# Threshold attention and a mixture of attention experts on one core: the same instructions from a new order table

## The chip, the core and the metric

The kernel runs on one core of a Trainium2 chip. The core has TensorE (PE in the profile; PEld is its weight load), VectorE (DVE), ScalarE (ACT), GpSimd (POOL) and SyncE (SP), which here only issues DMAs. ACT issues a few DMAs too. The engines run side by side, each works through its own list in order, and they wait for one another by semaphores. The metric is the device time of one execution in microseconds (us). Kernels are compared by the medians of their runs.

## The reference, cut to what matters

```python
# batch 8, heads 8, sequence S = 576, head_dim 64
scores = scale * q @ k.T                             # per batch and head
thresh = max(scores, -1) - tau                       # tau = 0.02
scores = where(scores >= thresh, scores, -1e9)
attn   = exp(scores - max); attn /= sum + 1e-9
x      = (attn @ v), heads side by side              # 8 x 576 x 512
logits = x @ w_gate                                  # 4 experts, the best 2 are used
for e in range(4):
    q, k, v = x @ wq[e], x @ wk[e], x @ wv[e]        # 512 -> 64
    a  = causal softmax(scale * q @ k.T)
    ye = a @ v @ wo[e]                               # 64 -> 512
    out += (weight of expert e in this row) * ye
```

All inputs and outputs are float32. The weights wq and wk are large (64 times the usual), so the products that lead to scores are computed in split precision.

## The kernel before, in words

The 64 heads are worked through as 32 pairs of two heads (n = 0 to 31). After every fourth pair one batch is complete, and its second half (projections, gate, expert attention, output) is put between the pairs that follow.

**One pair.** q and k are loaded (`ldq`, `ldk`: eleven DMAs a pair into one `qi` and one `ki` buffer, so the loads of pair n+1 wait until the transposes of pair n have read them), transposed on PE into PSUM (`tq`, `tk`, lines 1240 and 1103), and copied out as a high part rounded for the PE's fp32r mode and a low part (`kh`, `kl`, `qh`, `ql`; lines 1142, 1079 to 1087, 1155). For pairs 1 to 5 this takes three steps: a raw copy, a cast (line 1079, 1081 or 1083) and two halves of a subtraction (line 1087), which may run on POOL. The rows are then cut into five query tiles. A tile has a score matmul (`s`, names kk and qq, line 1103), and per head: the row minimum with a copy out of PSUM (`min`, DVE, line 1203), the exponential (`exp`, ACT, line 1216), the threshold with multiply and row sum (`stt`, DVE, line 1220), the reciprocal (DVE, line 1231), the scaling of the 576 columns (`pn`, line 1498 on POOL or DVE, 1496 on ACT), the transposition on PE (`tm`, line 1240), its copy out of PSUM (`pt`, line 1079 ACT or 1081 DVE), and the product with v (`av`). A small add (`thr`, `eps1`) stands ahead of stt and of the reciprocal (line 1074 DVE, 1211 ACT, 1213 POOL).

**One batch's second half.** x is split into high and low parts (`xh`, `xl`, `xd`), projected to q2 and k2 (`pj`) and to values and gate logits (`v`), the gate is computed in small steps, then causal scores (`s2`, `s2t`), row minimum (line 1470), exponential (1475, 1490), scaling (`p2s`), transposition (`t2`, line 1093), product with the values (`bv`), and the output projection with its store (`o`, `ob`, `st`).

**The weights** (`w`, `wh`, `wl`: load, cast to the high part, subtraction for the low part) are prepared beside the first four pairs; wo is woh and wol in the profile.

**What sets the order.** Nothing is ordered by loops. `work()` makes about 5,300 tasks, each with a name. `ORDER` gives each task its place, a number in one list over all engines, and `BY` gives the engine, as a digit, to each task that may run on several:

```python
by = int(BY[family][i]) if len(t) > 1 else 0
x = Task({...}, fn, deps, takes, uses, cols, ld, name, ORDER[family][i], by)
for t in sorted(tasks, key=lambda t: t.place):       # in plan()
```

`plan()` goes through the tasks by place, gives each its buffer, and emits them in that order; so the place decides where a task stands in the list of its engine. While the PE is still cold it also puts small matmuls on a constant (`tri`) between tasks, to keep it busy. The digits: for copies out of PSUM (`pt`, `kh`, `xr`) 0 is ACT and 1 is DVE; for casts (`xh`, `wh`, `qd`) 0 is POOL, 1 ACT, 2 DVE; for scalings (`pn`, `p2s`) 0 is POOL, 1 DVE, 2 ACT; for small adds and fences 0 is DVE, 1 ACT, 2 POOL; for subtractions (`xl`, `wl`, `kl`, `ql`) 0 is POOL and 1 is DVE.

Of the kernel before, what the change touches and what calls it, by code (L numbers as in the profile page):

```python
# [248 lines left out]
def work(K):  # L249
# [320 lines left out]
    for n in range(NPR):  # L570
# [18 lines left out]
        12,  # L589
    ],  # L590
    "tau": [
        11, 18, 20,
    ],
    "w": [
        397, 498, 508, 259, 198, 278, 281, 25, 21, 29, 227, 142, 271, 354, 555, 22, 460, 495, 79, 233, 357, 406, 568, 358, 384, 362, 471, 302, 335, 484,
    ],
    "wh": [
        552, 547, 299, 30, 61, 280, 180, 35, 502, 133, 319, 410, 447, 500,
    ],
    "wl": [  # L600
        574, 565, 331, 41, 109, 355, 246, 37, 505, 226, 336, 430, 462, 532,
    ],
    "ldk": [
# [7 lines left out]
    ],  # L611
    "ldq": [
# [6 lines left out]
    ],  # L619
    "ldv": [  # L620
# [20 lines left out]
    "qh": [
        15, 19, 62, 152, 300, 677, 618, 709, 776, 387, 531, 612, 835, 1321, 1329, 1389, 1466, 930, 1239, 1370, 1524, 1936, 1966, 2094, 2038, 1665, 1815, 2006, 2168, 2590, 2640,
        2744, 2795, 2307, 2502, 2574, 2864, 3311, 3294, 3367, 3395, 3037, 3192, 3334, 3399, 3951, 4019, 4048, 4085, 3746, 3800, 3979, 4101, 4587, 4569, 4670, 4694, 4258, 4503,
        4593, 4740, 5106, 5117, 5178, 5172,
    ],
# [8 lines left out]
    ],  # L654
    "fs": [
        33, 122, 240, 367, 516, 637, 806, 986, 1142, 1258, 1471, 1710, 1736, 1890, 2111, 2356, 2374, 2626, 2732, 2999, 3071, 3259, 3431, 3682, 3798, 3837, 4078, 4248, 4421, 4548,
        4697, 4885,
    ],
    "min": [
# [300 lines left out]
    "fs2t": "2202220211021222",  # L960
    "zh": "000100000000010000010010100000110000000101000010",
    "fo": "112010000110111122222002101101200100",
    "ob": "000001000000000100100000010000110000",
}


# [623 lines left out]
```

## Time and profile before

| | us |
|---|---|
| median of 3 runs | 817.98 (817.97 to 818.85) |
| the profiled execution | 816.84 |
| its span, first to last instruction | 815.1 (1.7 lie around it) |
| busy in the span: PE / PEld | 791.2 / 731.0 |
| DVE / ACT / POOL | 730.3 / 697.7 / 423.3 |
| TensorE's mean granted clock | 0.998 |

Busy time is the time in which an engine had at least one instruction in work. Matmuls are pipelined and their ends are modelled, so PE's busy time holds short waits; PEld shows them better. The chain of waits follows the work that ended last back to the start. Idle time of an engine that is not on it costs nothing.

### The profile page before, as it was taken

The numbers are of one execution on the slowest core, as the hardware profiler recorded it, in microseconds if no ns is written. First come the engines' busy times: TensorE is split into PE (matmuls) and PEld (weight loads), VectorE is DVE, ScalarE is ACT, GpSimd is POOL, SyncE is SP. The second block draws the span as 40 slices with busy tenths as digits, with TensorE's granted clock in tenths as the row PEclk, the third lists the DMA queues.
The fourth block names the chain that finished last, engine by engine and source line by source line (L and its number), as shares of the span: only waits on it lengthen the run. The fifth ranks groups of instructions, "written<-read, shape, count | busy, mean of one in ns | idle before, by whom it ended". The sixth has DMA issues, their size and how long they took to land.

```text
span 815.1 us, 34755 instructions
## 1 busy us (share of the span) xinstructions
PE 791.2 (97%) x14117; PEld 731.0 (90%) x14117; DVE 730.3 (90%) x2331; ACT 697.7 (86%) x1449; POOL 423.3 (52%) x811
## 2 busy tenths in 40 slices
PE   9888999999999999999999999999999999999998
PEld 7777898899988999888998999889998899988997
DVE  6999989998989989898989988998999988999584
ACT  5989888997899868998899988999999987999475
POOL 5998625753445345544365435455345563468232
PEclk9999999999999999999999999999999999999999
DMA  4433212112132112222222122202311212220002
GB/s 115 89 80 72 66 38 45 42 45 52 39 83 55 37 47 50 55 64 52 46 54 64 43 73 55 61 14 69 80 42 38 67 45 50 59 55 3 15 27 80
DMA packets 140240, 44.21 MB, mean 54 GB/s; under 512 B 135216, under 2 KB 135216, under 8 KB 140080
## 3 DMA queue, kind: packets, MB, share of 16 engines
q1 hardware_dynamic: 138512, 41.65, 20.9%
q8 instruction: 111, 1.82, 1.0%
q10 hardware_dynamic: 1568, 0.34, 0.2%
q14 instruction: 49, 0.40, 0.2%
HBM read 32.51 MB, written 9.44 MB: 51 GB/s over the span
## 4 chain that ended last, share of the span: by engine, by line
PE 76%; DVE 9%; ACT 6%; POOL 5%; issue 3%; DMA 1%; SPq 0%; DVEq 0%; ACTq 0%; POOLq 0%
PE ps L1103 64%; PE ps L1240 10%; DVE e L1203 3%; PE ps L1093 3%; POOL e L1498 2%; DVE e L1220 2%; ACT pt L1079 1%; ACT e L1216 1%; DMA ki<-in_k_dram 1%; ACT e L1475 1%; DVE e L1470 1%; POOL sm L1213 1%; ACT pa L1079 0%; DVE pt L1081 0%; ACT e L1490 0%
## 5 line engine op out<-in xcount | busy, mean ns | idle before, releaser
L1498 POOL TENSOR_SCALAR e<-e,sm 128x576 f32<-128x576 f32 (+4 forms) x277 | 193.5, 708 | 82.0 <-DVE sm L1231 55.3
L1203 DVE TENSOR_SCALAR_CACHE_REDUCE e<-ps 128x576 f32<-128x576 f32 x288 | 209.5, 752 | 21.2 <-PE ps L1103 15.5
L1216 ACT ACTIVATE e<-e,sm 128x576 f32<-128x576 f32 x288 | 215.3, 771 | 10.9 <-DVE e L1203 8.8
L1220 DVE SCALAR_TENSOR_TENSOR e<-e,sm,e 128x576 f32<-128x576 f32 x256 | 209.4, 841 | 2.4 <-ACT e L1216 0.7
L1103 PE MATMUL ps<-kk,qq 64*128 64x288 f32 x1900 | 176.1, 309 | 5.7 <-POOL kk L1087 1.3
L1103 PEld LDWEIGHTS ps<-kk,qq 64*128 64x128 f32 x1900 | 139.9, 186 | 16.1 <-DVE e L1203 3.4
L1079 ACT ACTIVATE pt<-ps 128x640 f32<-128x640 f32 (+3 forms) x228 | 142.5, 639 | 13.1 <-PE ps L1093 5.4
L1103 PE MATMUL ps<-pt,vm 128*64 128x128 f32 (+1 forms) x1536 | 143.9, 259 | 0.0
L1240 PE MATMUL ps<-ident,e 64*128 64x64 f32 x2624 | 123.8, 226 | 7.1 <-DVE e L1203 2.7
L1103 PEld LDWEIGHTS ps<-pt,vm 128*64 128x64 f32 x1536 | 127.3, 137 | 2.7 <-issue 0.7
L1240 PEld LDWEIGHTS ps<-ident,e 64*128 64x128 f32 x2624 | 108.8, 139 | 19.1 <-issue 5.1
L1103 PE MATMUL ps<-pa,vm 128*64 128x128 f32 x1024 | 124.4, 274 | 0.0
L1103 PEld LDWEIGHTS ps<-pa,vm 128*64 128x64 f32 x1024 | 110.7, 137 | 3.3 <-issue 1.2
L1103 PE MATMUL ps<-x,wh 64*128 64x288 f32 x1024 | 106.0, 296 | 0.0
L1213 POOL TENSOR_TENSOR sm<-sm 128x2 f32<-128x2 f32 (+1 forms) x127 | 41.9, 333 | 121.7 <-DVE e L1220 82.5
L1496 ACT ACTIVATE e<-e,sm 128x576 f32<-128x576 f32 (+4 forms) x116 | 83.2, 730 | 5.9 <-DVE sm L1231 4.8
L1103 PEld LDWEIGHTS ps<-x,wh 64*128 64x128 f32 x1024 | 84.2, 185 | 0.6 <-ACT kk L1142 0.2
L1103 PE MATMUL ps<-x,wl 64*128 64x288 f32 x512 | 78.5, 292 | 0.0
L1475 ACT ACTIVATE e<-e,sm 128x384 f32<-128x384 f32 (+3 forms) x128 | 70.9, 557 | 1.6 <-DVE sm L1470 1.0
L1079 ACT ACTIVATE pa<-ps 128x512 f32<-128x512 f32 x105 | 62.2, 595 | 7.0 <-PE ps L1240 6.8
L1470 DVE CUSTOM_DVE_ANT_0 e<-ps,tri 128x384 f32<-128x384 f32 (+3 forms) x128 | 58.4, 484 | 3.7 <-PE ps L1103 2.9
L1359 POOL TENSOR_SCALAR fencePOOL<-eps 128x2 f32<-128x2 f32 x56 | 16.7, 298 | 83.5 <-PE ps L1103 80.1
(153 smaller groups left out, 1656.5 us busy)
## 6 DMA issues: line engine op xcount, KB each, us to landing
vm<-in_v_dram SPq DMA_DIRECT2D x64, 128.0 KB, 2.6
out_dram<-ob SPq DMA_DIRECT2D x32, 256.0 KB, 2.4
ki<-in_k_dram SPq DMA_DIRECT2D x63, 80.0 KB, 2.5
qi<-in_q_dram SPq DMA_DIRECT2D x63, 80.0 KB, 2.5
ki<-in_k_dram SPq DMA_DIRECT2D x63, 64.0 KB, 2.4
vt<-in_v_dram SPq DMA_DIRECT2D x128, 16.0 KB, 2.2
qi<-in_q_dram SPq DMA_DIRECT2D x31, 64.0 KB, 2.4
qi<-in_q_dram SPq DMA_DIRECT2D x31, 48.0 KB, 2.4
```

Source lines behind the costliest of these rows:

```text
L1079: self.nc.scalar.activation(dst, src, AF.Copy)
L1093: self.nc.tensor.transpose(self.ps[:, bank, c * n:(c + 1) * n], x[sl], self.ident[sl, sl])
L1103: return self.nc.tensor.matmul(out, x, y, start=first, stop=last)
L1203: self.nc.vector.tensor_scalar(self.sides(sc), self.dbank(s)[:, :, :HS], 0.0, None, op0=ALU.add, op1=ALU.min, accum_out=self.small(sm)[:, ...
L1213: self.nc.gpsimd.tensor_tensor(m[:, to:to + n], m[:, of:of + 2 * n:2], m[:, of + 1:of + 2 * n:2], op=ALU.add)
L1216: self.nc.scalar.activation(self.row(e), self.row(sc), AF.Exp, bias=self.small(sm)[:, 2 * j:2 * j + 1], scale=-1.0)
L1220: self.nc.vector.scalar_tensor_tensor(self.row(e), self.row(sc), m[:, 8 + j:9 + j], self.row(e), op0=ALU.is_le, op1=ALU.mult, accum_out=m[ ...
L1240: self.nc.tensor.transpose(self.ps[:, g.slot + h, c * D:(c + 1) * D], x, self.ident[sl, sl])
L1470: self.nc.vector.tensor_tensor_reduce(self.row(p2)[:, :w], self.dbank(g)[:, j, :w], self.tri[:, SM - w:], 1.0, FAR, op0=ALU.add, op1=ALU.m ...
L1475: self.nc.scalar.activation(p, p, AF.Exp, bias=m[:, 2 * j:2 * j + 1], scale=-1.0, accum_out=m[:, 4 + 2 * j:5 + 2 * j])
L1496: self.nc.scalar.activation(p, p, AF.Copy, scale=x)
L1498: (self.nc.vector if e == "DVE" else self.nc.gpsimd).tensor_scalar(p, p, x, 0.0, op0=ALU.mult, op1=ALU.add)
```

## The change

The tables `ORDER` and `BY` have new numbers; every other line is the same. Of `ORDER` nearly every row differs, by a few places for most tasks (6 on average for a score matmul, 14 for a scaling) and by more for loads and stores. Of `BY` some 640 digits differ. The start of the diff, and its short rows:

```diff
     "warm": [
-        12,
+        16,
     ],
     "tau": [
-        11, 18, 20,
+        10, 19, 28,
     ],
...
 BY = {
-    "tau": "100",
-    "wh": "11011002211000",
-    "wl": "00000011000000",
+    "tau": "000",
+    "wh": "10111110101000",
+    "wl": "10000000000010",
...
-    "kh": "011002100001000100000100000000001",
+    "kh": "001100100000000100000110000010010",
...
-    "kl": "000000010000000000000000000000000000",
+    "kl": "000001000100000000000000000000000000",
```

By instructions, before and now: DVE 1,757 and 1,735; ACT 1,313 and 1,328; POOL 816 and 823; SP 599 and 599; PE the same 11,928 matmuls, and 89 and 93 small ones on `tri`. The 576-column scalings are 25 and 9 on DVE, 187 and 200 on POOL, 92 and 95 on ACT. The 512-column copies `pa` are 23 and 32 on DVE, 105 and 96 on ACT.

Three places are shown as they stand in the engine's list. The first is the start of DVE's list, from the copies of the first pair's q (qq) to the first row minima (L1203). Before:

```order
L1081 COPY qq_1_180<-ps 128x320
L1042 TENSOR_SCALAR sm<-tau_t 128x8x2
L1144 TENSOR_SCALAR kk_4_195<-ps,qsc 128x320
L1081 CAST woh<-ob_3_193 128x512
L1087 TENSOR_TENSOR wol<-ob_3_193,woh 128x512
L1203 TENSOR_SCALAR e_6_231,sm<-ps 128x576 x2
L1074 TENSOR_REDUCE sm<-sm 128x2
```

Now:

```order
L1081 COPY qq_2_190<-ps 128x320
L1042 TENSOR_SCALAR sm<-tau_t 128x8x2
L1203 TENSOR_SCALAR e_6_217,sm<-ps 128x576 x2
L1074 TENSOR_REDUCE sm<-sm 128x2
L1220 SCALAR_TENSOR_TENSOR e_7_236,sm<-e_6_217,sm,e_7_236 128x576
```

The scaled copy of kk went to ACT, which now does both halves in a row, and the cast and the subtraction of one half of wo (woh, wol) went to POOL.

The second is DVE's list at the end of the fourth pair, ahead of the 36th and last stt (L1220) of the first batch. x is that batch's split x, iv the copy that it is made from, wh the high part of a weight. Before:

```order
L1498 TENSOR_SCALAR e_99_1421<-e_99_1421,sm 128x576
L1203 TENSOR_SCALAR e_104_1468,sm<-ps 128x576 x2
L1081 CAST x_109_1510<-iv_95_1367 128x320
L1081 CAST wh_120<-ob_98_1408 128x256
L1220 SCALAR_TENSOR_TENSOR e_106_1500,sm<-e_96_1371,sm,e_106_1500 128x576
L1081 CAST x_109_1510<-iv_102_1449 128x256
L1220 SCALAR_TENSOR_TENSOR e_106_1500,sm<-e_96_1371,sm,e_106_1500 128x576
```

Now:

```order
L1081 COPY pa_102_1443<-ps 128x512
L1231 RECIPROCAL sm<-sm 128x2
L1203 TENSOR_SCALAR e_105_1490,sm<-ps 128x576
L1074 TENSOR_REDUCE sm<-sm 128x2
L1203 TENSOR_SCALAR e_105_1490,sm<-ps 128x576
L1220 SCALAR_TENSOR_TENSOR e_101_1427,sm<-e_97_1400,sm,e_101_1427 128x576 x2
```

The scaling, the three casts and other pieces left DVE here; a copy of pa came.

The third is POOL's list at the subtractions for the fourth pair's kk (kk_61, the low part of k). wh and wl are weights. Before:

```order
L1087 TENSOR_TENSOR kk_61_918<-pt_53_821,kk_61_918 128x320
L1213 TENSOR_TENSOR sm<-sm 128x2
L1087 TENSOR_TENSOR qq_63_936<-pt_50_787,qq_63_936 128x320
L1498 TENSOR_SCALAR e_58_870<-e_58_870,sm 128x576
L1087 TENSOR_TENSOR wl_125<-ob_54_823,wh_122 128x256
L1083 TENSOR_SCALAR wh_122<-sm 128x4
L1087 TENSOR_TENSOR wl_125<-ob_47_760,wh_122 128x256
L1083 TENSOR_SCALAR x_72_1030<-iv_71_1026 128x256
L1087 TENSOR_TENSOR kk_61_918<-pt_53_821,kk_61_918 128x320
```

Now:

```order
L1083 TENSOR_SCALAR kk_61_914<-pt_55_873 128x640
L1213 TENSOR_TENSOR sm<-sm 128x1
L1083 TENSOR_SCALAR wh_122<-sm 128x4
L1083 TENSOR_SCALAR qq_66_973<-pt_47_778 128x640
L1087 TENSOR_TENSOR qq_66_973<-pt_47_778,qq_66_973 128x320
L1087 TENSOR_TENSOR kk_61_914<-pt_55_873,kk_61_914 128x320
L1087 TENSOR_TENSOR qq_66_973<-pt_47_778,qq_66_973 128x320
```

Before, seven other pieces stood between the two halves of kk; now POOL does one half, close behind the cast, and the other half is on DVE.

In SP's list the six loads of the fifth pair's k end at place 72 before and at place 68 now; before, the last three stood right behind three loads of the same pair's q.

## Rows read from the trace of the kernel before

**Rows 1.** The page: span; busy us of each engine (share of the span), instructions.

```profile
span 815.1 us, 34755 instructions
...
PE 791.2 (97%) x14117; PEld 731.0 (90%) x14117; DVE 730.3 (90%) x2331; ACT 697.7 (86%) x1449; POOL 423.3 (52%) x811
```

**Rows 2.** Busy us of each engine by stretch, TensorE's granted clock, DMA share, GB/s.

```profile
core 0: us, PE busy (x) PEld busy (x) DVE busy (x) ACT busy (x) POOL busy (x), PEclk, DMA share, GB/s
...
40.00:62.00 22.00, 18.55 (x309) 16.18 (x306) 20.19 (x59) 18.29 (x33) 21.82 (x33) 0.92 0.39 86
100.00:760.00 660.00, 651.53 (x11888) 605.14 (x11887) 610.08 (x1969) 586.30 (x1227) 329.99 (x641) 1.00 0.21 50
```

**Rows 3.** The chain that ended last: shares of the span by engine.

```profile
PE 76%; DVE 9%; ACT 6%; POOL 5%; issue 3%; DMA 1%; SPq 0%; DVEq 0%; ACTq 0%; POOLq 0%
```

**Rows 4.** Columns as in rows 2: the first batch after its start.

```profile
24.00:61.00 37.00, 31.52 (x545) 27.55 (x543) 34.39 (x96) 33.00 (x61) 36.54 (x50) 0.96 0.38 84
61.00:90.00 29.00, 24.95 (x458) 21.71 (x454) 28.54 (x77) 24.83 (x45) 24.82 (x36) 0.99 0.31 69
```

**Rows 5.** The chain in order of time (start, us, what), 78 to 81 us.

```profile
77.79 0.62 DVE x L1081
78.41 0.41 DVE wh L1081
78.82 0.73 DVE e L1220 x2
79.56 0.74 DVE x L1081
80.30 0.74 DVE e L1220 x2
```

**Rows 6.** DVE's timeline: start us, us, line, operation, tiles [idle before <-releaser].

```profile
8.02 0.55 DVE L1144 TENSOR_SCALAR kk<-ps,qsc 128x320 f32<-128x320 f32 x1
8.81 0.43 DVE L1081 CAST woh<-ob 128x512 fp32r<-128x512 f32 x1 [0.26 <-DMA ob<-in_moe_wo_dram]
9.28 0.69 DVE L1087 TENSOR_TENSOR wol<-ob,woh 128x512 fp32r<-128x512 f32 x1
9.88 0.75 DVE L1203 TENSOR_SCALAR_CACHE_REDUCE e<-ps 128x576 f32<-128x576 f32 x1
```

**Rows 7.** Groups by line and form: busy us, mean ns of one | idle before <-releasers.

```profile
L1220 DVE SCALAR_TENSOR_TENSOR e<-e,sm,e 128x576 f32<-128x576 f32 x256 | 209.4, 841 | 2.4 <-ACT e L1216 0.7
...
L1498 POOL TENSOR_SCALAR e<-e,sm 128x576 f32<-128x576 f32 x187 | 144.4, 780 | 68.2 <-DVE sm L1231 55.3 <-DVE sm L1074 5.2 <-PE ps L1103 3.4
...
L1079 ACT ACTIVATE pa<-ps 128x512 f32<-128x512 f32 x105 | 62.2, 595 | 7.0 <-PE ps L1240 6.8
...
L1081 DVE COPY pa<-ps 128x512 f32<-128x512 f32 x23 | 15.6, 684 | 2.5 <-PE ps L1240 2.5
...
L1498 DVE TENSOR_SCALAR e<-e,sm 128x576 f32<-128x576 f32 x25 | 13.3, 535 | 0.3
...
L1081 DVE CAST kk<-pt 128x640 fp32r<-128x640 f32 x1 | 1.1, 1082 | 0.0
```

**Rows 8.** POOL's timeline, 48 to 57 us, columns as in rows 6.

```profile
48.80 0.87 POOL L1087 TENSOR_TENSOR kk<-pt,kk 128x320 fp32r<-128x320 f32 x1
...
55.06 1.35 POOL L1087 TENSOR_TENSOR kk<-pt,kk 128x320 fp32r<-128x320 f32 x1
```

**Rows 9.** PE's timeline, 56 to 60 us, columns as in rows 6.

```profile
56.47 0.54 PE L1103 MATMUL ps<-kk,qq 64*128 64x288 f32 x4 [1.34 <-POOL kk L1087]
...
58.04 0.82 PE L1240 MATMUL ps<-ident,ki 64*128 64x64 f32 x9 [0.67 <-DMA ki<-in_k_dram]
```

**Rows 10.** The stretch behind those waits, columns as in rows 2.

```profile
58.00:62.00 4.00, 3.89 (x45) 3.78 (x45) 2.19 (x10) 1.92 (x4) 3.82 (x6) 0.57 0.47 104
```

**Rows 11.** One line's instructions: duration ns min/median/max, first and last start.

```profile
L1220 DVE SCALAR_TENSOR_TENSOR e<-e,sm,e x256: 780/814/1417, 12.1 to 753.8; 128x576 f32<-128x576 f32 x128
```

More of the change, by code (lines that the diff above doesn't have):

```diff
@@ L768 @@
-        4799, 4976, 4971, 5045, 5074, 5091,
+        224, 354, 488, 526, 485, 489, 528, 580, 770, 729, 868, 1074, 975, 1090, 1213, 1221, 1430, 1543, 1539, 1631, 1829, 1793, 1848, 1895, 2066, 2221, 2343, 2244, 2374, 2470,
+        2519, 2544, 2729, 2785, 2880, 3081, 2966, 3060, 3172, 3198, 3559, 3464, 3581, 3589, 3768, 3764, 3846, 3864, 4095, 4196, 4287, 4416, 4419, 4473, 4491, 4502, 5060, 5028,
+        4977, 4810, 5074, 4997, 5071, 5088,
     ],
     "xl": [
-        499, 546, 581, 456, 543, 518, 566, 586, 917, 1049, 1231, 1193, 1224, 1226, 1218, 1235, 1820, 1862, 1750, 1654, 1854, 1872, 1864, 1893, 2536, 2386, 2351, 2337, 2524, 2522,
@@ L774 @@
+        5058, 4821, 5092, 5011, 5072, 5089,
     ],
     "xd": [
-        529, 587, 525, 545, 1047, 1143, 1185, 1221, 1759, 1570, 1817, 1859, 2354, 2380, 2446, 2546, 2916, 3171, 2973, 3197, 3539, 3823, 3797, 3859, 4409, 4235, 4435, 4525, 5084,
-        5080, 5078, 5075,
+        482, 534, 508, 538, 1001, 1047, 1083, 1226, 1718, 1876, 1832, 1880, 2522, 2366, 2413, 2529, 2740, 3092, 3178, 3203, 3560, 3790, 3853, 3859, 4436, 4389, 4514, 4511, 5083,
+        5031, 5093, 5073,
     ],
     "kr": [
-        81, 139, 258, 375, 559,
+        83, 148, 266, 359, 568,
@@ L781 @@
     ],
     "kl": [
-        104, 99, 195, 216, 301, 344, 413, 449, 592, 597, 619, 813, 979, 1134, 1304, 1463, 1690, 1841, 1953, 2139, 2332, 2506, 2591, 2722, 3030, 3164, 3239, 3406, 3664, 3818,
-        4004, 4067, 4238, 4440, 4664, 4745,
+        99, 103, 206, 200, 311, 334, 419, 422, 584, 599, 616, 810, 985, 1148, 1300, 1475, 1672, 1831, 1942, 2147, 2332, 2511, 2582, 2731, 3036, 3171, 3241, 3415, 3665, 3819,
+        3981, 4070, 4243, 4440, 4658, 4748,
     ],
     "qr": [
-        58, 132, 245, 372, 520,
+        58, 128, 235, 357, 505,
@@ L802 @@
+        2716, 2764, 2775, 3212, 3236, 3217, 3239, 3331, 3352, 3353, 3370, 3919, 3942, 3951, 3965, 4003, 4015, 4040, 4067, 4546, 4555, 4519, 4531, 4629, 4646, 4661, 4670, 5094,
+        5099, 5095, 5111, 5140, 5151, 5129, 5149,
     ],
     "fpj": [
-        610, 598, 676, 744, 1259, 1290, 1354, 1438, 1929, 1913, 2055, 1999, 2566, 2606, 2696, 2766, 3227, 3236, 3337, 3364, 3930, 3960, 4000, 4059, 4560, 4540, 4646, 4672, 5098,
-        5104, 5155, 5149,
+        607, 610, 676, 739, 1268, 1289, 1354, 1424, 1913, 1918, 2058, 2003, 2572, 2616, 2706, 2767, 3216, 3235, 3345, 3364, 3940, 3952, 4013, 4048, 4553, 4525, 4636, 4663, 5097,
@@ L818 @@
+        3890, 4561, 4586, 4591, 4605, 4589, 5110, 5116, 5106, 5113, 5100,
     ],
     "fv": [
-        654, 784, 1277, 1323, 1955, 1933, 2637, 2559, 3276, 3293, 3896, 3886, 4567, 4615, 5115, 5109,
+        644, 776, 1277, 1324, 1970, 1950, 2644, 2577, 3264, 3296, 3888, 3886, 4578, 4592, 5115, 5112,
     ],
     "v2": [
-        662, 801, 1298, 1356, 1983, 1950, 2652, 2575, 3282, 3317, 3923, 3910, 4598, 4626, 5123, 5124,
+        654, 800, 1307, 1338, 1976, 1972, 2659, 2594, 3275, 3307, 3906, 3921, 4588, 4622, 5124, 5127,
@@ L904 @@
+        5255, 5316, 5261, 5320,
     ],
     "zh": [
[L906 to L907 removed]
+        983, 989, 1056, 1093, 1082, 1112, 1597, 1594, 1615, 1676, 1674, 1765, 2237, 2231, 2396, 2350, 2347, 2414, 2910, 2912, 3013, 2998, 3011, 3075, 3583, 3584, 3688, 3606,
@@ L921 @@
+        5206, 5170, 5218, 5305, 5293, 5336, 5329, 5328,
     ],
     "ob": [
-        1137, 1144, 1217, 1244, 1722, 1874, 1827, 1804, 1902, 2370, 2798, 2491, 2461, 3102, 3165, 3124, 3109, 3174, 3645, 3792, 3768, 3843, 4433, 4408, 4471, 4466, 4520, 5096,
-        5228, 5187, 5234, 5315, 5306, 5331, 5339, 5335,
+        1142, 1147, 1243, 1248, 1722, 1867, 1836, 1811, 1898, 2389, 2806, 2489, 2462, 3101, 3146, 3128, 3102, 3176, 3648, 3792, 3778, 3842, 4431, 4402, 4471, 4465, 4535, 5098,
+        5221, 5193, 5233, 5314, 5299, 5339, 5335, 5332,
@@ new lines @@
+    "qh": "11000010010000100010111100000101000001101000101100000120001000202",
+    "fs": "12201220110211101112022220200102",
+    "thr": "2212021212000201000021221221002112000102200000212201222010022112200002100020021011010200000020020222010120121122102212122102110200002220022220201110001020202000",
+    "eps1": "2212102122221101202022112112020112012220122012202201201121021001120202020220222202200001220010012201220002100100002022121201120222202222020112212211001222222222",
+    "pn": "000020022002220000000220002002020102202222022020020020002000000020000002202022020002000200020000000022201020002010220202000000020000000000020020020000212202200002002000200220202020000220220222220000000000010200000002020220220222000002002000002000022021002000220222001200200000000022000102",
@@ new lines @@
+    "pt": "010000001000000000000000000010000000011001000010100100010000100000001000101010000010100001000100010000011010110000100001000100001000000000000010000000010100101000110000000001000000000000000001000000011000000010000010000000000000000101010000010001000010010000001000101110010000010001000101",
+    "xr": "0000000000000000001000000000000000100001010100000000110100000010",
+    "xh": "0001001210100101111000110200121111200200011100021001022221010012",
+    "xl": "0101011100001011000101000100001000001000110000010000000111001011",
@@ L963 @@
-    "ob": "000001000000000100100000010000110000",
+    "ql": "0000000001000010100010000001000011000000000000000000000000001000000000110000000011000000000000111011",
+    "fpj": "21212112000202111201210121112020",
+    "qu": "00000010100010000000000100001000",
+    "qd": "01002101110012001000001201110001",
+    "fv": "0000221210100221",
+    "v2": "0010010000011000",
+    "shr": "11111110111001110111111111011001101111100100000110101111100011101110001000110100",
+    "p2s": "000000000000000022221220000000200220000100012000010022200220000000020020100000212000020200000000200200202020120000000000202211000012001000002000",
@@ L964 @@
+    "pt2": "0000011100000001000000010000000000000000000000100001000010000000000000000000000010010000000000001010001000111000",
+    "fs2t": "0102020112122212",
+    "zh": "010010000000001000100000000000000000000000011000",
+    "fo": "222201202102111020121201121100101210",
+    "ob": "000011000010000101000000000000000000",
 }
```

122 lines of the change are left out of this document (47 added, 75 removed), and 304 rows, old and new, of the table ORDER.

## The prediction

> **What bounds the kernel now.** I read the busy times first. PE is busy for 791.2 of 815.1 us, DVE for 730.3, ACT for 697.7, POOL for 423.3 [rows 1]. Then the chain of waits: PE holds 76% of it, DVE 9%, ACT 6%, POOL 5% [rows 3]. So PE sets the time over most of the span, and PE's matmuls are the same before and after. What an order can change is the time that PE stands still or runs below its clock, and that is not spread evenly, which the busy times by stretch show. From 100 to 760 us PE is busy for 651.53 of 660 us, with DVE at 610.08 and ACT at 586.30 behind it [rows 2]: 8.5 us of 660 stand open. From 24 to 90 us PE is busy for 31.52 of 37.00 and 24.95 of 29.00, so 9.5 us of 66 stand open, and there another engine has no gaps: POOL works 36.54 of the 37.00, DVE 28.54 of the 29.00 [rows 4]. This first batch, where the weights are prepared beside the first pairs, is where pieces taken off an engine can shorten the kernel one for one. Later a piece taken off DVE mostly makes DVE wait a little longer for PE.
>
> The sum below is made against the profiled execution, 816.84 us (the span and 1.7 around it); the median of the runs is 817.98, so 1.14 is added at the end.
>
> **The change part by part: the first batch.** I take DVE's list up to the 36th stt, the last of that batch, which runs at 80 us. These pieces left it: at the start the scaled copy of kk (0.55), the cast woh (0.43) and the subtraction wol (0.69) [rows 6]; one cast of kk (1.08) and one scaling (0.54) [rows 7]; at the end two casts of x and one of wh. The chain runs through those last three for 0.62, 0.41 and 0.74 [rows 5], but the two of x were drawn out by what stood beside them; I count 0.41 for each, 1.2 together. That is 4.5. One copy of pa came (0.68 [rows 7]), and small ones, which by their kinds nearly cancel (a subtraction of a weight gone; a subtraction of x and a fence come; about +0.2 net, an estimate). So DVE has 3.6 us less to do before the 36th stt.
>
> What of it shows? At the end of the batch nearly all of it should, since DVE is busy there without a break and the chain passes through it: 77.79 to 80.30 is DVE alone, one step after another [rows 5]. At the start woh and wol stand directly ahead of the first row minimum, which starts at 9.88 when wol ends [rows 6], so 1.1 us comes off in front of the first tile; of that ACT gives back a part, because it now does the two halves of kk in a row where DVE and ACT shared them. POOL takes woh and wol over. DVE's 1.12 for the two would be 1.6 there by the ratio of the two engines' scalings (780 to 535 ns [rows 7]), an estimate, and POOL has only 0.46 of free time between 24 and 61 [rows 4]. That is a price which cuts the gain.
>
> In the middle of the batch PE waited 1.34 us for the second half of kk from POOL and 0.67 for the loads of ki [rows 9]. POOL's two halves start at 48.80 and 55.06, though both have one input [rows 8]; the seven pieces between them are the cause. The new order puts one half right behind the cast and gives the other to DVE, so I expect this wait to go. The ki loads stand four places earlier in SP's list, so that wait should shrink. In the 4 us behind these waits PE's granted clock is 0.57, about the lower of its two levels (1.2 of 2.4 GHz), with PE busy for 3.89 [rows 10]: 4.0 x 0.43 = 1.7 us is lost to it. Together PE could win 3.7 us here. But DVE was idle for only 1.81 of the 22 us from 40 to 62 [rows 2], so if DVE has the same work, at most 1.8 can be won before DVE is late next. And POOL, with 21.82 of 22 [rows 2], may be late before that.
>
> Ends for the first batch: nothing (POOL's added work and the next queue eat all), and -3.6 - 1.8 = -5.4. I take **-3.0**: DVE's own reduction, less what ACT and POOL take back at the start, with nothing counted for the middle.
>
> **The change part by part: the rest.** By counts and mean durations, over the whole program: DVE has 16 fewer scalings at 535 ns (-8.6) and 9 more copies pa at 684 (+6.2) [rows 7]; the other forms, each below 3 us, come to -6.9; so -9.3 in all, of which -3.6 is counted above and -5.7 remains. ACT loses the 9 copies at 595 (-5.4) [rows 7] and gains +9.4 in many small forms, so +4.0. POOL gains 13 scalings at 780 (+10.1) [rows 7] and +1.9 of others, so +12.0. I weigh each by the engine's share of the chain [rows 3], since I can't say which of these pieces end a wait: DVE -5.7 x 9% = -0.5, ACT +4.0 x 6% = +0.2, POOL +12.0 x 5% = +0.6. What hides POOL's added work is its idle time, 330 of 660 us free between 100 and 760 [rows 2]. If that cover fails, a scaling that moved from DVE to POOL takes 0.25 us longer (780 - 535): 13 of them are 3.2 us. If DVE's -5.7 shows in full it is -5.7. These are the ends for the rest: -5.7 and +3.2, and I take +0.3.
>
> Sum: -3.0 + 0.3 = -2.7. That is 814.1 for the profiled execution and **815.3** for the median.
>
> **A rule that speaks against it.** DVE and POOL disturb each other: the stt (line 1220) takes between 780 and 1417 ns, with 814 in the middle [rows 11] and 841 on the mean [rows 7], so 256 x 27 ns = 6.9 us are lost in its long cases. The Trainium skill says why ("SBUF — State Buffer", section "Who interferes with whom"): the two engines have one pair of SBUF ports in common, held as an exclusive lock, and whoever comes second stands still until the other is done. By that rule each scaling moved to POOL can stop a DVE instruction that needs both ports, for as long as it lasts; the trace agrees in kind, since the longest stt is 637 ns over the shortest, most of a POOL scaling. By the rule alone the sum would be the rival below; by the rows the loss was a small part of what 187 scalings on POOL could have cost, 6.9 of 144.4 us.
>
> **Rivals.** *Larger gain.* DVE is a second bound everywhere, not just at first: 610 of 660 us leave it little room [rows 2], and each short wait that the chain takes through DVE costs PE. Then the ends add up: -5.4 in the first batch, -5.7 for the rest, +0.8 for ACT and POOL; -10.3, or 807.7 on the median. Halfway, -6.5, is 811.5. For it: both waits of PE at 56 to 58 us have a cause that the new order takes away. Against: from 100 to 760 us only 8.5 us of PE's time stand open, and the number of tiles that DVE must serve is the same.
>
> *No change.* POOL, which has 0.46 us free of 37 [rows 4], is late next in the first batch by as much as DVE is earlier, and the rest is hidden behind PE: -0.3 to +0.6, or 817.7 to 818.6. For it: POOL gets the pieces that DVE loses at the start. Against: in 61 to 90 us POOL is busy for only 24.82 of 29.00 [rows 4], and there DVE alone is full.
>
> *Slower.* The 13 scalings that POOL gains between 100 us and the end each stop DVE for their whole length: 13 x 0.78 = 10.1 us. DVE wins 5.7 there by its smaller list, so it ends 4.4 later; with the start's -3.0 and +0.8 of ACT and POOL this is +2.2, or 820.2; without the start's gain, 823. It decides as soon as more than about 9.5 of the 10.1 us is lost. For it: DVE has only 50 us of 660 free. Against: the 187 scalings there now cost 6.9 us in stt, so 13 more should cost 0.5.
>
> **How the numbers follow.** What a measurement of this kernel can tell from no change is about 0.2%, 1.6 us. Forecast (-1 to -5, so 813 to 817): 0.42. Larger gain: 0.20. No change: 0.18. Slower, by this mechanism or by a start in which POOL loses more than DVE gains: 0.20. Of the forecast's cases a few fall within 0.2%, and a few of the "no change" ones fall outside it on either side, which leaves faster 0.60, same 0.19, slower 0.21. The range takes in the larger gain nearly to its end and the slower case past its centre: 808 to 822. Its ends leave out about 1 in 10 on each side. The forecast's own range is 813 to 817.
>
> **What would show it.** In the profile after: the first row minimum starts about 1 us before 9.88; the wait of 1.34 on POOL's kk is gone and the clock does not fall to half behind it; the 36th stt starts near 77 instead of 80.30, and every later landmark is earlier by the same amount, neither growing nor shrinking between 100 and 760 us. DVE's busy time is near 721, POOL's near 435. The mean of the stt stays within 10 ns of 841. The forecast is wrong if the 36th stt is not earlier (then POOL's list was the bound in the first batch), if the lead grows by several us after 100 us (then DVE was a bound there), or if it shrinks, with the mean of stt above 860 (then the shared ports decide).

## The result: slower by 0.59%, and the profile after

| | before | after |
|---|---|---|
| median of 6 runs each, us | 817.98 (816.21 to 818.85) | 822.42 (822.04 to 823.87) |
| ratio, 95% interval | | 1.0059 (1.0046 to 1.0072) |
| span of the profiled execution | 815.1 | 820.0 |

The forecast was 815.3, with a range up to 822. The page after (span, busy time, the chain by engine):

```profile
span 820.0 us, 34787 instructions
...
PE 793.1 (97%) x14121; PEld 731.4 (89%) x14121; DVE 727.8 (89%) x2309; ACT 698.2 (85%) x1464; POOL 429.2 (52%) x818
...
PE 71%; DVE 11%; ACT 6%; POOL 3%; issue 2%; DVEq 0%; POOLq 0%; ACTq 0%
```

DVE's busy time fell by 2.5 us, POOL's rose by 5.9 and ACT's by 0.5 [rows 1]. The directions are those of the forecast, the sizes are not: it counted -9.3, +12.0 and +4.0. PE has the same matmuls in both profiles, form by form: 14,028 beside those on `tri` (not the 11,928 named with the change). DVE's share of the chain rose all the same, from 9% to 11% [rows 3]. By stretch (columns as in rows 2):

```profile
24.00:61.00 37.00, 32.21 (x555) 28.00 (x554) 34.88 (x99) 32.97 (x60) 33.61 (x45) 0.95 0.43 96
61.00:90.00 29.00, 25.01 (x438) 21.56 (x436) 28.50 (x76) 25.97 (x49) 28.00 (x43) 0.94 0.32 69
100.00:760.00 660.00, 649.72 (x11835) 603.36 (x11831) 609.36 (x1953) 583.99 (x1227) 330.25 (x642) 1.00 0.21 51
44.00:48.00 4.00, 3.08 (x42) 3.08 (x44) 2.09 (x8) 3.85 (x7) 3.97 (x6) 0.68 0.33 74
84.00:88.00 4.00, 3.33 (x52) 2.78 (x53) 4.00 (x9) 2.87 (x6) 4.00 (x7) 0.80 0.47 106
```

From 61 to 90 us POOL now has hardly a gap either: 28.00 of 29.00, where it had 24.82 [rows 4]; DVE is as full as it was. From 24 to 61 us POOL has 2.93 us less than before. From 100 to 760 us PE is busy for 1.8 us less of the 660 than before [rows 2], DVE for 0.7, ACT for 2.3, and POOL for 0.3 more. And there are two stretches at a reduced clock, 0.68 and 0.80, where before there was one [rows 10].

To set traces side by side, each matmul of PE is weighed by its shortest spacing in a dense stretch, and the moments are compared at which two programs have started the same weight. The lateness against the first profile of the kernel before, in us, at seven such moments (named by their time in that profile); the kernels of the last columns come below:

| moment | after | after again | before again | start_before | start_after | a_act | a_light | b_light | a_mend |
|---|---|---|---|---|---|---|---|---|---|
| 9.3 | 1.3 | 3.3 | 0.2 | 0.2 | 3.6 | 1.9 | 1.7 | -0.3 | 0.5 |
| 54.5 | 3.7 | 4.2 | 0.4 | 2.0 | 5.1 | 3.1 | 4.3 | 2.5 | 2.4 |
| 99.3 | 1.2 | 3.1 | -1.1 | 1.1 | 1.8 | -0.1 | 1.4 | 1.6 | -1.2 |
| 120.2 | 1.8 | 3.7 | -1.1 | 1.6 | 2.2 | 0.5 | 2.0 | 1.6 | -0.7 |
| 413.6 | 1.8 | 3.6 | -1.1 | 1.5 | 1.8 | -0.2 | 1.7 | 1.1 | -1.4 |
| 592.2 | 3.9 | 5.7 | -1.1 | 4.2 | 1.9 | 1.5 | 3.2 | 0.8 | -0.3 |
| 810.8 | 4.8 | 6.6 | -0.7 | 5.6 | 2.1 | 2.7 | 3.6 | 0.5 | 0.8 |

Read down the column "after": 1.2 us are lost in the first 99 us, with large swings in between, and 3.6 behind them, in small steps. The columns "after again" and "before again" are second profiles of the same two kernels; up to 99 us they differ from the first ones by up to 2.0 us. So a difference of 1 or 2 us there, in one profile, need not be the kernel's.

**The start.** PE's timeline after, where k's last block is transposed and the first score matmul runs:

```profile
8.74 0.27 PE L1240 MATMUL ps<-ident,ki 64*128 64x64 f32 x1 [0.90 <-DMA ki<-in_k_dram]
...
9.82 1.73 PE L1103 MATMUL ps<-kk,qq 64*128 64x288 f32 x12
```

The same score matmul in PE's timeline before:

```profile
8.49 1.84 PE L1103 MATMUL ps<-kk,qq 64*128 64x288 f32 x12
```

The first score matmul starts 1.33 us later, because PE waits for a load of k. ACT issues that load last, behind four loads of q, as ACT's queue after shows (start, us in the queue):

```profile
0.80 2.73 ACTq L1106 DMA_DIRECT2D qi<-in_q_dram  x4
4.00 1.55 ACTq L1106 DMA_DIRECT2D ki<-in_k_dram  x2
```

This is no single execution's. In all eight profiles of kernels with the changed first loads (most of them come below) the first score matmul starts at 9.58 to 11.28 us, and in five of them the granted clock from 8 to 16 us is down to between 0.57 and 0.79. In the seven profiles of kernels that start like the kernel before it starts at 8.14 to 8.77, always at a clock of 1.00.

DVE stands idle until the first row minimum, for PE and not for anything of its own list (DVE's timeline after):

```profile
11.11 0.76 DVE L1203 TENSOR_SCALAR_CACHE_REDUCE e<-ps 128x576 f32<-128x576 f32 x1 [3.73 <-PE ps L1103]
```

**The end of the first batch.** The chain after, in order of time (start, us, what), runs through POOL:

```profile
77.60 2.22 POOL x L1083 x3
79.82 0.84 POOL x L1087
81.75 0.78 POOL x L1087
82.53 1.21 POOL wl L1087
83.74 0.74 POOL e L1498
```

PE's timeline after has the wait at its end:

```profile
84.53 1.08 PE L1240 MATMUL ps<-ident,e 64*128 64x64 f32 x28 [1.83 <-POOL e L1498]
```

DVE came earlier, by half of what was counted: its 36th stt starts at 78.57, before at 80.22. In the kernel before PE waited at this place too, but for DVE (PE's timeline before):

```profile
84.84 0.53 PE L1240 MATMUL ps<-ident,e 64*128 64x64 f32 x10 [1.44 <-DVE e L1203]
```

That wait went, and one for POOL came: the scaling that PE needs next now stands in POOL's list behind three casts and two subtractions of x and pieces of the weights. PE waited 1.83 us for it, and the clock fell behind the wait. The second profiles show the same exchange, 1.45 us for DVE before and 1.82 for POOL after. POOL is not late because of more work: up to 90 us it was busy for 75.6 us before and 77.3 after, in the second profiles for 77.3 and 75.2. The order of its list is new.

**At 43 us.** ACT stood for the load of a weight, ahead of its cast, as ACT's timeline after shows:

```profile
43.31 0.42 ACT L1079 ACTIVATE wh<-ob 128x256 fp32r<-128x256 f32 x1 [1.52 <-DMA ob<-in_moe_wv_dram]
```

PE stood for a copy behind that cast (PE's timeline after):

```profile
44.92 0.74 PE L1240 MATMUL ps<-ident,ki 64*128 64x64 f32 x10 [1.74 <-ACT pa L1079]
```

**The rest.** PE's weight loads show its waits best. From 105 to 785 us the waits with an engine as releaser sum up to 21.9 us in 80 waits before (DVE 5.5, ACT 10.7, POOL 5.7) and to 24.5 us in 88 after (DVE 10.2, ACT 7.9, POOL 6.4); the second profiles give 21.9 and 24.5 again. The groups that grew (us in total, times, longest), 105 to 760 us, before:

```profile
PEld ps L1240 <- POOL e L1498: 1.8, 7, 0.6
...
PEld ps L1103 <- DVE pt L1081: 0.3, 1, 0.3
```

The same view after:

```profile
PEld ps L1240 <- POOL e L1498: 3.4, 10, 0.7
...
PEld ps L1103 <- DVE pt L1081: 1.5, 2, 0.9
PEld ps L1103 <- DVE fenceDVE L1359: 1.2, 2, 0.8
```

So while DVE's busy time hardly changed (0.7 us less from 100 to 760), PE waited 4.7 us longer for it, and 2.8 us less for ACT. The longest of these waits in DVE's timeline after:

```profile
416.27 1.49 DVE L1220 SCALAR_TENSOR_TENSOR e<-e,sm,e 128x576 f32<-128x576 f32 x1
...
417.79 0.78 DVE L1081 COPY pt<-ps 128x640 f32<-128x640 f32 x1
```

In POOL's timeline after, at the same time:

```profile
416.28 1.66 POOL L1087 TENSOR_TENSOR x<-iv,x 128x320 fp32r<-128x320 f32 x2 [1.63 <-ACT x L1079]
```

And in that of PE's weight loads:

```profile
418.62 0.82 PEld L1103 LDWEIGHTS ps<-kk,qq 64*128 64x128 f32 x12 [0.89 <-DVE pt L1081]
```

The stt takes 1.49 us instead of 0.81, beside two subtractions of POOL, the copy pt stands behind it, and PE waits 0.89 us for the copy. The Trainium skill ("SBUF — State Buffer", section "Who interferes with whom") would name the ports that DVE shares with POOL; the rows agree with it at this place, where the two overlap, but no run shows that the ports are the cause. Over all, the stt is hardly longer than before [rows 7, 11], 845 ns on the mean, with this spread after (ns min/median/max):

```profile
L1220 DVE SCALAR_TENSOR_TENSOR e<-e,sm,e x256: 778/814/1493, 12.9 to 756.9; 128x576 f32<-128x576 f32 x128
```

### The profile page after: what moved, and what is told of

It is laid out like the page before. It is cut to its first block, busy times and chain, and to the rows that moved or that the text cites. A ratio compares the mean times of both kernels' runs of the same rounds, so it can differ in the third digit from the quotient of the medians.

```text
span 820.0 us, 34787 instructions
## 1 busy us (share of the span) xinstructions
PE 793.1 (97%) x14121; PEld 731.4 (89%) x14121; DVE 727.8 (89%) x2309; ACT 698.2 (85%) x1464; POOL 429.2 (52%) x818
## 3 DMA queue, kind: packets, MB, share of 16 engines
q8 instruction: 111, 1.82, 0.9%
## 4 chain that ended last, share of the span: by engine, by line
PE 71%; DVE 11%; ACT 6%; POOL 3%; issue 2%; DVEq 0%; POOLq 0%; ACTq 0%
PE ps L1103 59%; PE ps L1240 9%; DVE e L1220 3%; DVE e L1203 3%; PE ps L1093 2%; POOL e L1498 2%; ACT pt L1079 2%; ACT e L1216 1%; ACT e L1475 1%; DVE e L1470 1%; DVE pt L1081 1%; DVE z L1087 0%; DVE sm L1231 0%; POOL sm L1213 0%; POOL x L1083 0%
## 5 line engine op out<-in xcount | busy, mean ns | idle before, releaser
L1498 POOL TENSOR_SCALAR e<-e,sm 128x576 f32<-128x576 f32 (+4 forms) x286 | 201.2, 711 | 99.2 <-DVE sm L1231 76.5
L1203 DVE TENSOR_SCALAR_CACHE_REDUCE e<-ps 128x576 f32<-128x576 f32 x288 | 208.2, 751 | 22.1 <-PE ps L1103 18.5
L1220 DVE SCALAR_TENSOR_TENSOR e<-e,sm,e 128x576 f32<-128x576 f32 x256 | 210.2, 845 | 4.0 <-ACT e L1216 1.5
L1079 ACT ACTIVATE pt<-ps 128x640 f32<-128x640 f32 (+3 forms) x234 | 145.2, 638 | 7.7 <-PE ps L1093 3.3
L1213 POOL TENSOR_TENSOR sm<-sm 128x2 f32<-128x2 f32 (+1 forms) x132 | 39.5, 300 | 121.0 <-DVE e L1220 68.2
L1496 ACT ACTIVATE e<-e,sm 128x576 f32<-128x576 f32 (+4 forms) x127 | 88.9, 712 | 6.9 <-DVE sm L1231 5.4
L1103 PEld LDWEIGHTS ps<-x,wh 64*128 64x128 f32 x1024 | 87.5, 185 | 0.5 <-DVE e L1203 0.3
L1103 PE MATMUL ps<-x,wl 64*128 64x288 f32 x512 | 82.1, 292 | 0.0
L1475 ACT ACTIVATE e<-e,sm 128x256 f32<-128x256 f32 (+3 forms) x128 | 70.9, 557 | 2.8 <-DVE sm L1470 2.4
L1470 DVE CUSTOM_DVE_ANT_0 e<-ps,tri 128x256 f32<-128x256 f32 (+3 forms) x128 | 58.6, 485 | 6.7 <-PE ps L1103 3.4
L1079 ACT ACTIVATE pa<-ps 128x512 f32<-128x512 f32 x96 | 56.3, 593 | 4.0 <-PE ps L1240 3.3
L1103 PE MATMUL ps<-wh,x 64*128 64x260 f32 x576 | 59.6, 283 | 0.0
```

The source lines that it names most:

```text
L1079: self.nc.scalar.activation(dst, src, AF.Copy)
L1103: return self.nc.tensor.matmul(out, x, y, start=first, stop=last)
L1203: self.nc.vector.tensor_scalar(self.sides(sc), self.dbank(s)[:, :, :HS], 0.0, None, op0=ALU.add, op1=ALU.min, accum_out=self.small(sm)[:, ...
L1213: self.nc.gpsimd.tensor_tensor(m[:, to:to + n], m[:, of:of + 2 * n:2], m[:, of + 1:of + 2 * n:2], op=ALU.add)
L1220: self.nc.vector.scalar_tensor_tensor(self.row(e), self.row(sc), m[:, 8 + j:9 + j], self.row(e), op0=ALU.is_le, op1=ALU.mult, accum_out=m[ ...
L1470: self.nc.vector.tensor_tensor_reduce(self.row(p2)[:, :w], self.dbank(g)[:, j, :w], self.tri[:, SM - w:], 1.0, FAR, op0=ALU.add, op1=ALU.m ...
```

## The experiments

Unless said otherwise, times are medians of 4 to 12 runs beside runs of the kernel before on the same chip; a ratio is to these. The changed kernel's ratio lies between 1.0046 and 1.0072. Where a variant's interval overlaps this one, the times alone do not tell the two apart, and what is said rests on one profile.

**Each wait of the first batch by itself.** First the loads:

```diff
 the changed kernel
-ACT: qi 3, qi 4, qi 5, qi 5, ki 5, ki 4        SP: ki 4, qi 1, ki 1, ki 5, tau, ki 1
+ACT: qi 4, qi 3, qi 5, ki 4, ki 5, tau         SP: qi 1, ki 5, qi 5, ki 1, ki 4, ki 1
```

(The number behind qi or ki is the blocks of 64 x 64 in that load.)

> The changed kernel, with the twelve loads of the first pair (k, q and tau) in the order and on the two queues of the kernel before; all later lists as changed. In the changed kernel the first score matmul starts at 9.82 us, in the kernel before at 8.49, because the fourth-block load of k sits last in ACT's queue and lands at 8.7. Theory A (each wait of the first batch costs PE and is kept to the end): first score matmul near 8.5, time about 1.2 us below the changed kernel, 821.2. Theory B (DVE and POOL without gaps up to 90 us take it back): first score matmul near 8.5, but less than 0.4 us of it left at 100 us, time 822.4.

821.28 us, ratio 1.0045 (1.0029 to 1.0062). The first score matmul starts at 9.13, and the lateness at 99 us is 0.15 instead of 1.2. That is theory A by the size of the gain, though the intervals overlap and 9.13 is not the 8.5 of both theories; the 3.6 us behind are not touched (4.2 late at the end). With these loads the first score matmul starts at 9.02 to 9.13 in the three changed kernels that have them. What is left to 8.5 is for the most part ACT, which now copies both halves of kk in a row; in a_mend below PE waits for the second one (PE's timeline):

```profile
9.02 1.73 PE L1103 MATMUL ps<-kk,qq 64*128 64x288 f32 x12 [1.02 <-ACT kk L1142]
```

```diff
 the changed kernel, ACT's list
+pn 128x576, pa 128x512, pt 128x640
 wh<-ob 128x256
-pn 128x576, pa 128x512, pt 128x640
```

> The changed kernel, with the cast of one weight (wh, from in_moe_wv) on ACT three places later, behind a scaling and two copies. In the changed kernel ACT stood 1.52 us for this weight's load ahead of the cast (43.31 us), PE then waited 1.74 us, and from 44 to 50 us the granted clock is 0.50 to 0.86. Theory A: the wait and the half clock go, about 3 us earlier at 50 us, and 1 to 3 us of it are left at the end: 819.4 to 821.4. Theory B (another queue is late next): PE waits elsewhere, clock still falls within 15 us, time 822.4 within 0.5.

823.08 us, ratio 1.0073 (1.0056 to 1.009). The wait for ACT's copy went, and PE waited 1.21 and 0.77 us for scalings of POOL at 49 and 51 us and 2.17 us for a fence on DVE at 63 us instead. Theory B.

```diff
 the changed kernel
-pn[34] on POOL
+pn[34] on DVE
```

> The changed kernel, with one scaling of 576 columns (the one that POOL starts at 83.73 us behind x casts, x subtractions and weight pieces) on DVE. In the changed kernel PE waits 1.83 us for it and from 86 to 90 us the granted clock is 0.55 to 0.60. Theory A: the wait and the half clock go, time 2 to 3 us below the changed kernel, 819.4 to 820.4. Theory B (the next piece of POOL's list or DVE's is late instead): clock still falls, time 822.4 within 0.5.

821.26 us, ratio 1.0047 (1.0029 to 1.0064): 1.2 us less on the median, half of what theory A gave, and the intervals overlap. The wait for POOL went. In its place PE waited 0.85 us for DVE's row minimum, and the clock still fell (0.70 from 84 to 88 us, 0.87 from 88 to 92).

The three together:

> The changed kernel with the three edits together (first pair's loads as before, the weight cast three places later, the one scaling on DVE). Theory A: first 100 us shorter by 4 to 5.5 us than in the changed kernel, time 817 to 818.5, so the loss of the change is these three waits and what they do to the clock. Theory B (each is replaced by another wait in a batch in which three engines have no gaps): less than 1.5 us, time above 821.

821.33 us, ratio 1.0049 (1.0033 to 1.0065). 1.1 us below the changed kernel, where the three by themselves would make -1.1 + 0.7 - 1.2 = -1.6: theory A fails for the three taken together, and theory B holds. The wait at 43 us went, and PE waited for a fence on DVE instead (PE's timeline):

```profile
59.42 2.03 PE L1103 MATMUL ps<-kk,qq 64*128 64x288 f32 x18 [1.80 <-DVE fenceDVE L1359]
```

The same wait stands in a_wv (2.17 us) and in the second profile of the changed kernel (1.88), which also lack the one at 43 us.

**First batch or rest.** Two kernels with one list up to about 100 us and the other behind it:

```diff
-places of one kernel
+tasks of the first 721 (648) places by one kernel, all others by the other, with the engines that belong to them
```

> The first 721 tasks (to about 105 us) in the order and on the engines of the kernel before, the rest in the order and on the engines of the changed kernel. In the profiles the changed kernel is 1.2 us late at 100 us and 4.8 at the end, so 3.6 come after the first batch. Theory R (the loss is mostly in the rest, as many short stalls of PE): about 3.6 us above the kernel before, 821 to 822. Theory S (the first batch sets it, the rest only hands it on or reacts to it): within 1.2 us of the kernel before, below 819.2.

822.32 us, ratio 1.0056 (1.0041 to 1.0072). Theory R: it loses 4.0 us behind 120 us, where the changed kernel loses 3.0. The 1.1 us at 99 are not the list's: up to there the lists are those of the kernel before, but in this profile PE waited for a load of ki at 26.8 us, which it had not done, and the clock fell to 0.60 from 28 to 32 us (PE's timeline):

```profile
26.83 0.71 PE L1240 MATMUL ps<-ident,ki 64*128 64x64 f32 x10 [1.34 <-DMA ki<-in_k_dram]
```

Two other profiles of kernels that have these lists up to there, b_light and b_fix below, show the same wait (1.55 and 1.51 us) and clock (0.57 and 0.68); four others do not. So it comes and goes from execution to execution.

> The first 648 tasks (to about 100 us) in the order and on the engines of the changed kernel, the rest as in the kernel before. Theory R: 1.2 us above the kernel before, about 819. Theory S: 3 us or more above it, 821 to 823.

819.63 us, ratio 1.0026 (1.0013 to 1.0039): 2.1 us for the first batch of the changed kernel, between the two theories by time; by the profile it is R, since behind 120 us the lateness stays at 1.8 to 2.2 to the end.

**Order or engines.**

```diff
-ORDER and BY of one kernel
+ORDER of one, BY of the other
```

> The order of the kernel before with the engine choices of the changed one (13 more scalings on POOL, 16 fewer on DVE). Theory E (the engines chosen cost the time: PE waits for scalings that are late on POOL): 2 to 5 us above the kernel before, 820 to 823, and PE's waits for POOL's scalings grow as in the changed kernel. Theory O (the order costs it): within 1.6 us of the kernel before.

942.54 us, ratio 1.153. (783 digits of `BY` differ between the two kernels, more than the 640 named with the change.)

> The changed kernel's order, and its engines up to place 647 (about 100 us); from there the engine choices of the kernel before in all families but the scalings of the second half (p2s). Theory E: the 3.6 us that the changed kernel loses after 100 us go, time about 819. Theory O: they stay, 822 or more, since an order made for other engines can only gain waits.

913.49 us, ratio 1.117. Both expectations miss by far, and neither theory is decided: a place is only right for the engine it was made for. Where the two are mixed, PE waits everywhere; the longest sum in the first of the two (columns as above):

```profile
PE ps L1240 <- POOL e L1498: 10.5, 13, 2.1
```

**POOL's scalings in DVE's way.** In both kernels:

```diff
 scalings on POOL, of pn and p2s, after place 700
-p = all columns of its row (128 to 576)
+p = its first 2 columns
```

This cuts 253 scalings of the kernel before and 260 of the changed one, 163 and 174 of them of 576 columns; the other columns stay unscaled.

> The kernel before, with the scalings on POOL after place 700 (about 105 us) cut to 2 of their columns, so that the other columns stay unscaled: POOL hardly holds the ports that it has in common with DVE for them. To be compared with the same cut in the changed kernel. Alone it should be 0 to 3 us faster than the kernel before, by fewer long stt and fewer waits for POOL (5.7 us of PE's waits before).

816.66 us, ratio 0.9978 (0.9966 to 0.999).

> The changed kernel with the same cut: the scalings on POOL after place 700 cut to 2 columns, the rest unscaled. Theory L (POOL's scalings in DVE's way, 13 more of them, cost the 3.6 us after 105 us): between 105 us and the end the two cut kernels differ by less than 1.2 us. Theory Q (where pieces stand in DVE's list costs it, whatever POOL does): they differ by 2.5 to 4.5 us as the uncut ones do.

820.14 us, ratio 1.0028 (1.0014 to 1.0042). From 99 us to the end the first wins 1.2 us on its uncut kernel (lateness 1.6 to 0.5), the second 1.4 (3.6 us lost become 2.2). Between the two cut kernels 3.4 us remain behind 99 us, of 3.6: theory Q. POOL's scalings cost either kernel a little over 1 us, and not the difference; whether by standing in DVE's way or by coming late for PE is not told apart. POOL's subtractions, which stand beside the stretched stt at 416 us, were not cut: their results are read, so that was not tried.

**PE's waits for DVE.**

```diff
 the changed kernel
-pt[74], pt[153], fs2t[6], fo[17] on DVE
+on ACT
```

> The changed kernel with four small choices turned from DVE to ACT: the two copies of pt that PE waits for 0.60 us at 208 and 0.89 at 418, and the two fences that it waits for 0.82 at 426 and 0.34 at 480. After 105 us two programs with one order have kept their distance within 0.3 us, so the lateness against the changed kernel at 500 us is read from the profile. Theory W (PE's waits for DVE are added one by one): 1.3 to 2.6 us earlier than the changed kernel at 500 us, and the same at the end. Theory N (ACT, busy for 586 of 660 us, is late next): less than 0.6 us earlier at 500 us.

822.08 us, ratio 1.0056 (1.004 to 1.0072), so by time nothing is seen; its runs spread from 819.96 to 823.13. By the profile, which is of the fastest of them, from 120 to 592 us it loses 1.0 us where the changed kernel loses 2.1. Between the theories: around the first three pieces it wins 1.6 us on the changed kernel (0.7 at 208 us, 0.9 from 418 on), and 0.5 is lost again between 436 and 482 us, around the fourth.

**Stretches.** The kernel before with two stretches of the changed one:

> The kernel before, with two stretches (320 to 384 us and about 604 to 694 us) in the order and on the engines of the changed kernel, in which the changed kernel won 1.2 and 0.9 us on the kernel before. Theory T (each stretch brings its own stalls, and they add): 1.5 to 2.5 us faster than the kernel before. Theory C (the changed kernel only caught up there, because it was late): within 0.8 us of the kernel before.

820.05 us, ratio 1.0034 (1.0021 to 1.0048), slower than the kernel before. At the first seam, from 322 to 345 us, it lost some 1.7 us, more than the stretch then won. Theory T fails as put; the seams make it no clean test of theory C.

**The same kernels once more.**

> The kernel before, unchanged, once more with a profile: what of its first 100 us repeats. Theory P (the waits of PE at 56 and 58 us and the half clock behind them belong to the program): PE again waits about 1.3 us for POOL's kk near 56 us, the clock is near 0.6 from 58 to 62, and no point of the first 100 us moves by more than 0.5 us. Theory V (loads that land now earlier, now later move the first batch from run to run): the waits sit elsewhere, and points of the first 100 us move by 1 to 3 us, while the way from 105 us to the end keeps its length within 0.3 us.

816.11 us. Half of each theory. The waits came again, as PE's timeline in the new profile shows (its last line is a wait that the first profile did not have):

```profile
56.82 0.53 PE L1103 MATMUL ps<-kk,qq 64*128 64x288 f32 x4 [1.32 <-POOL kk L1087]
...
58.31 0.58 PE L1240 MATMUL ps<-ident,ki 64*128 64x64 f32 x9 [0.58 <-DMA ki<-in_k_dram]
...
70.73 0.46 PE L1240 MATMUL ps<-ident,e 64*128 64x64 f32 x8 [1.48 <-POOL e L1498]
```

The fall of the clock did not come (58 to 62 us, columns as in rows 2):

```profile
58.00:62.00 4.00, 3.42 (x59) 3.31 (x61) 3.52 (x12) 3.39 (x6) 4.00 (x7) 1.00 0.64 142
```

The moments behind 62 us moved by 1.1 us for it, and the way from 99 us to the end kept its length within 0.3.

> The changed kernel, unchanged, once more with a profile. Theory P: the waits at 43.2 and 82.7 us and the two stretches at half clock behind them come again. Theory V: other waits, points of the first 100 us moved by 1 to 3 us, the way from 105 us to the end the same within 0.3 us, so that the part of the loss that always comes is the 3.0 to 3.6 us behind 105 us, and the first batch only adds 1 to 2 us on the mean. In both the first score matmul starts late, near 9.8 us, since the order of the first loads is the program's.

823.95 us. The wait for ki at the start and that for POOL's scaling at 86.66 (1.82 us) came again; the one at 43 us did not, and the one for DVE's fence came instead (1.88 us at 62 us). Neither theory in full. The first one in PE's timeline of the new profile:

```profile
8.52 0.52 PE L1240 MATMUL ps<-ident,ki 64*128 64x64 f32 x6 [1.54 <-DMA ki<-in_k_dram]
```

Here it was followed by the lower clock (8 to 16 us, columns as in rows 2):

```profile
8.00:16.00 8.00, 7.05 (x42) 5.83 (x44) 2.83 (x9) 3.18 (x7) 3.76 (x5) 0.59 0.56 142
```

Behind 99 us it lost 3.4 us, after 3.6 in the first profile.

**All that had helped, together.**

```diff
 the changed kernel
-loads of the first pair; pn[34] on POOL; pt[74], pt[153], fs2t[6] on DVE
+loads as before; pn[34] on DVE; pt[74], pt[153], fs2t[6] on ACT
```

> The changed kernel with the first pair's loads as before, the one scaling of the first batch on DVE, and three of the four DVE pieces that PE waited for on ACT (two copies of pt, the fence at 426 us; the fence at 480 us stays on DVE, because on ACT it cost 0.3 us). Theory W (named waits add): 1.1 of the loads, 1.1 of the scaling and 1.3 of the three pieces off, so 818.5 to 819.5. Theory N (the queue behind each gives it back): above 820.5.

818.47 us, ratio 1.0009 (0.9996 to 1.0021), clear of the changed kernel's interval. Theory W: of the 4.4 us over the kernel before 1.0 is left, each against its own runs of that kernel. Twelve loads and four pieces of 5,341 tasks carried most of the loss, taken together; no single one of them is shown by time. PE's wait at 43 us is still there (2.21 us), so it is no part of this.

**The term of the forecast by itself.**

```diff
 the kernel before
-kl[5] (second half of the fourth pair's kk) on POOL
+on DVE
```

> The kernel before with one digit changed: the second half of the subtraction for the fourth pair's kk, which POOL starts at 55.06 us behind seven other pieces and for which PE waited 1.32 to 1.34 us in both profiles, on DVE (that part of the change alone). Theory W (a wait that repeats is worth its length): 1.0 to 1.4 us earlier behind 58 us than the same kernel without it, kept to the end, 816.1 to 816.7. Theory N (DVE, 20.19 of 22 us busy there, or the loads of ki behind it are late next): less than 0.5 us.

817.46 us, ratio 0.9998 (0.9987 to 1.0009). Theory N, and by more than it named. Of the wait 0.36 us is left, now for DVE; the next, for the load of ki, is 0.91 instead of 0.58; and two later waits for POOL's scalings are longer (PE's timeline):

```profile
62.92 0.77 PE L1240 MATMUL ps<-ident,e 64*128 64x64 f32 x18 [1.06 <-POOL e L1498]
...
70.73 0.46 PE L1240 MATMUL ps<-ident,e 64*128 64x64 f32 x8 [1.77 <-POOL e L1498]
```

In the second profile of the kernel before, which also kept its clock, these were 0.52 and 1.48. At 62 us this kernel is 0.5 us ahead of that profile, at 74 us level with it: nothing of the 1.32 us is left.

> The same, and one scaling of the fourth pair (on POOL at 68.69 us, for which PE waited 1.48 us in the second profile of the kernel before, and not in the first) on ACT. Theory W: 1 to 2 us below the kernel before, 815.5 to 816.7. Theory N: within 0.8 us of the kernel before.

817.38 us, ratio 0.9996 (0.9987 to 1.0005). Theory N. No kernel here is faster than the one before beyond its interval, but for the one that leaves work out.

## Why the prediction was wrong, step by step

**The first batch, -3.0: the step that failed.** "At the end of the batch nearly all of it should [show], since DVE is busy there without a break and the chain passes through it." What was measured is +1.2 us at 99 us, and +3.1 in the second profile. DVE's 36th stt came 1.65 us earlier, half of the 3.6, and in the second profiles 1.57 us later, behind a later start. PE's wait for DVE at that place did go (1.44 us), but the chain does not follow DVE, it follows whichever engine is late: PE then waited 1.83 us for a scaling on POOL. POOL went from 24.82 to 28.00 of 29.00 there, and from 36.54 to 33.61 of 37.00 ahead of it, so it was for the most part its own work, moved later. The "no change" rival had this mechanism (POOL late next) and argued against it with the 24.82 of before, which is no room in the new list. With that scaling on DVE (a_pn) PE waits 0.85 us for DVE. b_kk shows the same in one piece: a wait taken from PE where the next engines have no gap is a wait later.

**The start, -1.1 of it.** The row said that the first row minimum starts when wol ends, 9.88. It did not say that PE would have allowed it earlier. After, where DVE has nothing else to do, it starts 1.29 us behind the first score matmul (9.82 and 11.11); by that distance it could have started at 9.78 before (8.49 + 1.29, an estimate). So woh and wol hid 0.1 us. What set the start was the order of the first loads, which the forecast did not look at: +1.3 in the first profile and +3.3 in the second, where the clock fell as well. With the loads as before the first score matmul starts at 9.02 to 9.13 instead of 9.58 to 11.28; the rest to 8.5 is for the most part what ACT "gives back", which the forecast had named.

**The middle, counted at nothing.** The wait for kk did go, and rightly nothing was counted for it: other waits came in its place (1.74 us at 43 us, or 1.88 for DVE's fence at 62). The half clock of [rows 10], which I priced at 1.7 us as a possible gain, was one execution's: the second profile of the kernel before has the waits without it.

**The rest, +0.3: measured +3.4 to +3.6, the second step that failed.** The bounds were -5.7 and +3.2. The amounts of work were not there to be weighed: from 100 to 760 us DVE's busy time fell by 0.7 us and not 5.7, POOL's rose by 0.3 and not by up to 12.0. And an engine's work times its share of the chain does not give a time: with nearly the same work DVE let PE wait 4.7 us longer, where a copy or a fence that PE needs stood behind long pieces. Three of them turned to ACT gave back 1.6 us of the 3.6 (a_mend, from 99 us to the end). The other 2.0 are many small steps, which were not assigned one by one.

**The slower rival** had the right sign and the wrong cause. The stt's mean rose by 4 ns, less than the 10 that the prediction set as its sign, and without POOL's scalings the difference stayed. POOL's subtractions, which stand beside the longest stt, were not tested.

**What stays open.** Why the load of ki at 26.8 us comes late in some executions of the old lists; how much of the first batch's 1.2 to 3.1 us comes in the average run (2.1 by start_after, with an interval from 1.1 to 3.2); and which of the edits of a_mend is worth what.

## What to carry to other kernels

Work taken off a full engine is only a gain if no other engine is late next in that very stretch: lay the new list of every engine over it before counting anything, for old gaps are no room in a new order. For the first matmul follow the loads, by queue and issue time, before the engines. In a dense stretch look not at how much an engine does, but at what stands directly ahead of the few pieces that TensorE waits for; here turning a few of them, and the first loads, gave back most of what moving thousands had lost.

## What was not expected of the hardware

The same program moved by 1.1 and 1.9 us within its first 99 us from one profile to the next, and hardly behind them (0.3 and 0.2). Two things moved. The loads landed at other times: after, the transposes of ki at the start began at 7.11 in one execution and at 8.52 in the other. And the granted clock differed: it fell to 0.59 (the lower level, 1.2 of 2.4 GHz) behind a wait of 1.54 us at 8.5 us in one execution, and stayed at 1.00 behind waits of 0.81 and 0.90 us at the same place in another.
